# Stacked queries in two buffers in turn from the 17th pair on, with their split written half a step earlier

## Chip, cores and metric

The kernel runs on one core of one Trainium2 chip. The metric is the device time of one execution in microseconds (us). The kernel before takes 730.91 us (median of three executions, 730.74 to 735.16).

## What is computed

Windowed attention with a few sink positions, followed by a gated feed-forward layer. There are 4 batches, 8 heads, 768 positions and 64 numbers per head; a query sees the first 4 positions and the last 128 up to its own. In short:

```
scores = q @ k^T / 8                      # per batch and head, 768 x 768
keep   = (col < n_sink) | (0 <= row - col < window)
a      = softmax(where(keep, scores, -1e9))
x      = (a @ v) laid out as 3072 x 512
h      = x @ w_in                         # 3072 x 2048
out    = (h * clip(h + 3, 0, 6) / 6) @ w_out
```

## The kernel before

**Tiling.** The tokens are cut into 12 units of 256 positions (4 batches, 3 units each; the first unit of every batch comes first). A unit has 4 pairs of heads, so 48 pairs, numbered s = 0 to 47 below; the 17th pair is s = 16. For one pair TensorE computes four score blocks (two heads h, two halves t of 128 queries; `C_score`, L293), VectorE (DVE) masks them and takes the minimum, ScalarE (ACT) does the exponentials and the scaling (`C_soft`), TensorE transposes the probabilities (`D_pt`) and multiplies them with v (`E_av`). When the four pairs of a unit are done, the unit's feed-forward steps go into a queue: for each of 8 slices of the hidden layer two steps of 12 matmuls (`ffn1`, L467, into `hps`), and a slice later two steps of 6 wider matmuls (`ffn2`, L487, into `o`); at the end two steps (`ffn_out`) that hold no matmul, only a copy on ACT and a store. Between the two kinds of matmul the activation runs as a chain: ACT `gf` (L473), DVE `gf` (L474), DVE `gh` (L41), DVE `g` (L476).

**Split numbers.** TensorE reads rounded 32-bit numbers, so operands are split into a high and a low part. For the queries of pair s, `B_q` (L266) lets ACT write the high part and DVE the low part into `qt` (one buffer), and then four DMAs on SyncE's queue (SP) stack the parts of each head on top of each other in the tile `Q` (one buffer, L272). `B_k` (L253) does the same for the keys: `kt`, and four larger DMAs into `K` (one buffer). The score matmuls of pair s read K and Q of pair s. Pairs 0 to 9 take another, plain path without Q and K. The raw queries `qr` and keys `kr` have two buffers each and are loaded from HBM one step ahead by `A_kq`.

**What sets the order.** One list, `ORDER` (L564), is run once per step s: "V" loads and splits v, C00 to C11 are the four scores of pair s-1, E0 and E1 the products with v of pair s-2, "L" loads q and k of pair s+1, "Bk" and "Bq" stack the keys and queries of pair s, D0, D1 and S are transposes for pair s-1. Each "-" takes one step from the feed-forward queue, so there are eight of them in a pair. That is the written order; the framework that builds the program then places ready work of one engine ahead of work that isn't ready, so that an engine's final order differs a little from the written one. Each engine and SP's queue work strictly in their final order, and a DMA waits on SP's queue until its source is written and its destination is free.

**Buffers that matter here.** `Q` and `K` of pair s can only be written when the last score of pair s-1 (C11) has read the old ones. `qt` can only be written again when the four DMAs that read it have landed. The tag `st` (three buffers of 4 KB per partition) holds the staged weights at the start, up to step 11, and afterwards only the output tile `ost` of `ffn_out` (L492).

Of the kernel before, what the change touches and what calls it, by code (L numbers as in the profile page):

```python
# [10 lines left out]
F32R = mybir.dt.float32r  # L11
# [7 lines left out]
P = 128  # L19
# [7 lines left out]
def split_parts(nc, hi, lo, src, hi_engine, lo_engine):  # L27

    copy_r(nc, hi_engine, hi, src)
    lo_engine.tensor_tensor(out=lo, in0=src, in1=hi.bitcast(F32), op=ALU.subtract)  # L30
# [14 lines left out]
def attn_ffn_kernel(ctx: ExitStack, tc: tile.TileContext, qx, kx, vx, vfx, vsx, n_sink, window, w_in, w_out, out):  # L45
# [4 lines left out]
    H, D, UT = 2 * NP, 64, 256  # L50
    S = NU * UT
# [5 lines left out]
    work = fast.enter_context(tc.tile_pool(name="work", bufs=2))  # L57
# [125 lines left out]
    def later_constants():  # L183

        bias_from(m_t0[:, 0:P], prev, nc.gpsimd)
        bias_from(m_t0[:, P:2 * P], own, nc.gpsimd)
        bias_from(m_t0[:, 2 * P:W2], snk[:, 0:SK], nc.gpsimd)
        nc.gpsimd.tensor_copy(out=m_t1[:, 0:P], in_=m_t0[:, 0:P])
        nc.gpsimd.tensor_copy(out=m_t1[:, P:P + SK], in_=m_t0[:, 2 * P:W2])
        nc.gpsimd.tensor_copy(out=m_t1[:, P + SK:W2], in_=m_t0[:, P:2 * P])  # L190
        nc.gpsimd.memset(pz.bitcast(F32), 0.0)
# [15 lines left out]
    def eng(which, s):  # L207
        return {"D": nc.vector, "P": nc.gpsimd, "A": nc.scalar}[which[1 + (s % (len(which) - 1)) if s < START else 0]]
# [16 lines left out]
    def plain(s):  # L225
        return s < NF32 and pus[s][1] == 0
# [26 lines left out]
    def B_k(s):  # L253
# [9 lines left out]
                                  in_=kt[D * h:D * (h + 1), :, 0:w].bitcast(F32))  # L263
        st_[s]["K"] = K

    def B_q(s):  # L266
        if plain(s):
            return
        d = st_[s]
        qt = work.tile([P, 2, UT], F32R, name="qt", bufs=1)  # L270
        split_parts(nc, qt[:, 0, :], qt[:, 1, :], d["qr"], eng(QHI, s), eng(QLO, s))
        Q = work.tile([P, 2, UT], F32R, name="Q", bufs=1)  # L272
        for h in range(2):
            for r in range(2):
                nc.sync.dma_start(out=Q[D * r:D * (r + 1), h, :].bitcast(F32),
                                  in_=qt[D * h:D * (h + 1), r, :].bitcast(F32))
        d["Q"] = Q

# [14 lines left out]
    def C_score(s, h, t):  # L293
# [15 lines left out]
        else:  # L309
            K, Q = d["K"], d["Q"]  # L310
            for part in range(2):
                nc.tensor.matmul(out=sp[:, 0:w], lhsT=Q[:, h, t * P:(t + 1) * P],  # L312
                                 rhs=K[:, h, part, k0c:k0c + w], start=(part == 0), stop=(part == 1))
# [198 lines left out]
    NS = len(pus)  # L512
    queues = []

    def drain(n):

        for _ in range(n):
            live = [q for q in queues if q]
            if not live:
                return  # L520
            if live[0] is queues[0] and len(live) > 1:
                order = live[0:2]
            else:
                order = live[0:1]
            for q in order:
                if q[0][0] <= 4 * NFP - len(w_order):
                    q.pop(0)[1]()
                    break
# [16 lines left out]
    def slot_C(s, h, t):  # L545
        if 0 <= s < NS:
            C_score(s, h, t)
            if t == 1:
                C_soft(s, h)
                if s == 0 and h == 1:  # L550
                    keep_busy(WARM[1])
                elif 0 < s < NP:
                    keep_busy(WARM[2])
# [7 lines left out]
                dsts = [out[r0 + P * tt:r0 + P * (tt + 1), :] for tt in range(2)]  # L561
                queues.append(ffn_steps(units.index((b, u)), xt[(b, u)], work, ps, ps, dsts, "bank"))

    ORDER = "V C00 - C01 - C10 - C11 E0 L - Bk E1 - Bq W - D0 - D1 S -"  # L564
    MULT = [1] * 12
    WN = [0, 1, 1, 1, 1, 4, 4, 4, 4, 4, 4, 4]

    for s in range(NS + 2):
        if s == 3:
            later_constants()  # L570
        for step in ORDER.split():
            if step == "-":
                drain(MULT[s] if s < len(MULT) else 1)
            elif step[0] == "C":
                slot_C(s - 1, int(step[1]), int(step[2]))
            elif step[0] == "E":
                slot_E(s - 2, int(step[1]))
            elif step == "V":
                if s < NS:
                    A_v(s)  # L580
                if 2 <= s and pus[s - 2][1:] == (1, 0):
                    batch_loads(pus[s - 2][0])
            elif step == "L" and s + 1 < NS and s > 0:
                A_kq(s + 1)
            elif step == "Bk" and 0 < s < NS:
                B_k(s)
            elif step == "Bq" and 0 < s < NS:
                B_q(s)
            elif step == "W":
                for _ in range(WN[s] if s < len(WN) else 0):  # L590
                    with ExitStack() as behind:
                        if s <= 5:
                            at = max(min(s, NP) - 2, 0)
                            behind.enter_context(tc.issue_after(st_[at]["min"].ins))
                            behind.enter_context(tc.issue_after(st_[at]["exp"].ins))
                        w_order.pop(0)()
            elif step[0] == "D" and 0 <= s - 1 < NS:
                D_pt(s - 1, int(step[1]))
            elif step == "S" and 0 <= s - 1 < NS:
                D_snk(s - 1)  # L600
# [169 lines left out]
```

## Time and profile before

| | |
|---|---|
| median of three executions | 730.91 us (730.74 to 735.16) |
| the profiled execution, its own time | 730.63 us |
| its span (first to last instruction) | 728.9 us |
| TensorE matmul busy | 709.6 us, 97% of the span |
| DVE busy | 495.4 us, 68% |
| ACT busy | 426.3 us, 58% |
| DMA: K stacking, Q stacking | 152 issues each |

The profile is one execution, taken by the hardware profiler. PE is TensorE's matmul side and PEld its weight loads; SPq is SyncE's DMA queue. A number in square brackets behind a row of a timeline is the time in which the engine sat idle before that instruction, with the name of what ended the wait. A matmul's shown length is longer than the distance at which matmuls follow each other, because they are pipelined: a wait of PE is best read from the distance between two starts.

### The profile page before, as it was taken

To read this page: it belongs to the slowest core of one execution; us is meant where nothing else is said; L and a number is where in the kernel's file an instruction comes from. 1 tells how busy PE (TensorE), PEld (TensorE's weight loads), DVE (VectorE), ACT (ScalarE), POOL (GpSimd) and SP (SyncE) were. 2 spreads that over 40 slices of the span, in tenths; PEclk is the share of its full clock that TensorE was granted. 3 is DMA by queue.
4 is the path that set the end of the run, shared out by engine and by line. 5 is a ranking of instruction groups with operands and counts; after the bars stand their busy time and mean duration, and the time that the engine had idled before them with its cause. 6 is when DMAs were issued, how large, how long until landed. Compare 5 with 4: busy or idle time off the path is not lost.

```text
span 728.9 us, 14295 instructions
## 1 busy us (share of the span) xinstructions
PE 709.6 (97%) x4772; PEld 635.8 (87%) x4772; DVE 495.4 (68%) x1418; ACT 426.3 (58%) x1139; POOL 169.6 (23%) x336
## 2 busy tenths in 40 slices
PE   8997999999999999999999999999999999999996
PEld 7776788998999998999898899999899899899995
DVE  5798999666876766876866876776776775533321
ACT  6988997656566656665555665755655754311111
POOL 1000000000233433433443343353343342100000
PEclk9999999999999999999999999999999999999999
DMA  7656583535546436436445635545635522000000
GB/s 238 196 185 229 194 255 93 152 89 137 146 103 174 116 97 178 127 96 166 115 106 129 175 97 126 152 108 136 167 99 129 150 72 61 30 1 1 30 1 33
DMA packets 55601, 89.11 MB, mean 122 GB/s; under 512 B 8416, under 2 KB 38368, under 8 KB 55520
## 3 DMA queue, kind: packets, MB, share of 16 engines
q1 hardware_dynamic: 55376, 88.11, 44.1%
q8 instruction: 40, 0.66, 0.4%
q14 instruction: 41, 0.34, 0.1%
q10 hardware_dynamic: 144, 0.00, 0.0%
HBM read 42.47 MB, written 6.29 MB: 67 GB/s over the span
## 4 chain that ended last, share of the span: by engine, by line
PE 79%; DVE 7%; ACT 5%; DMA 5%; issue 2%; SPq 1%; POOL 0%; ACTq 0%; DVEq 0%; POOLq 0%
PE hps L467 32%; PE o L487 31%; PE av L429 6%; PE sp L312 5%; PE pt L362 3%; DMA K<-kt 2%; PE sp L307 2%; SPq L262 1%; DMA Q<-qt 1%; DVE gf L474 1%; DVE g L476 1%; ACT Pt L336 1%; DMA st<-in_w_out_dram 1%; ACT gf L473 1%; PE idle L81 1%
## 5 line engine op out<-in xcount | busy, mean ns | idle before, releaser
L467 PE MATMUL hps<-xh,wih 128*128 128x256 f32 x768 | 220.8, 288 | 3.5 <-DVE st L160 2.3
L467 PE MATMUL hps<-xh,wil 128*128 128x256 f32 x768 | 217.3, 283 | 0.2 <-DVE wil L165 0.2
L467 PE MATMUL hps<-xl,wih 128*128 128x256 f32 x768 | 216.1, 282 | 0.1
L487 PE MATMUL o<-woh,gh 128*128 128x512 f32 x384 | 155.1, 404 | 3.7 <-DVE gh L41 3.6
L487 PE MATMUL o<-woh,g 128*128 128x512 f32 x384 | 152.2, 399 | 0.8 <-DVE g L476 0.4
L467 PEld LDWEIGHTS hps<-xh,wih 128*128 128x128 f32 x768 | 144.7, 188 | 8.1 <-ACT wih L35 5.9
L487 PE MATMUL o<-wol,gh 128*128 128x512 f32 x384 | 151.4, 394 | 0.0
L467 PEld LDWEIGHTS hps<-xl,wih 128*128 128x128 f32 x768 | 144.9, 189 | 1.1 <-DVE xl L445 0.3
L467 PEld LDWEIGHTS hps<-xh,wil 128*128 128x128 f32 x768 | 144.4, 188 | 0.9 <-DVE wil L165 0.4
L336 ACT ACTIVATE Pt<-Pt,nb 128x272 f32<-128x272 f32 (+2 forms) x152 | 77.0, 507 | 74.0 <-DVE nb L314 73.0
L344 POOL TENSOR_TENSOR Pt<-Pt 128x256 f32<-128x256 f32 x64 | 47.3, 739 | 276.0 <-ACT Pt L336 276.0
L473 ACT ACTIVATE gf<-hps,three 128x512 f32<-128x512 f32 x96 | 65.4, 682 | 77.1 <-PE hps L467 76.4
L474 DVE SCALAR_TENSOR_TENSOR gf<-gf,hps 128x512 f32<-128x512 f32 x96 | 65.9, 686 | 62.6 <-ACT gf L473 59.5
L487 PEld LDWEIGHTS o<-woh,g 128*128 128x128 f32 x384 | 72.2, 188 | 20.7 <-DVE g L476 4.7
L487 PEld LDWEIGHTS o<-woh,gh 128*128 128x128 f32 x384 | 72.4, 189 | 15.6 <-DVE gh L41 3.8
L487 PEld LDWEIGHTS o<-wol,gh 128*128 128x128 f32 x384 | 72.5, 189 | 10.5
L322 ACT ACTIVATE Pt<-Pt,rc 128x144 f32<-128x144 f32 (+2 forms) x152 | 55.7, 414 | 43.2 <-POOL Pt L344 38.9
L476 DVE TENSOR_TENSOR g<-gf,gh 128x512 fp32r<-128x512 f32 x96 | 68.8, 716 | 1.2 <-PE o L487 0.3
L380 POOL TENSOR_SCALAR_AFFINE_SELECT ph<-ph 128x256 fp32r<-128x256 f32 x64 | 32.5, 512 | 155.7 <-ACT ph L35 155.7
L314 DVE CUSTOM_DVE_ANT_0 Pt<-sp,m_t 128x272 f32<-128x272 f32 x128 | 54.8, 432 | 17.8 <-PE sp L312 15.8
L312 PE MATMUL sp<-K,Q 128*128 128x272 f32 (+2 forms) x304 | 61.7, 287 | 2.0 <-DMA Q<-qt 1.9
L312 PEld LDWEIGHTS sp<-K,Q 128*128 128x128 f32 x304 | 51.5, 189 | 9.7 <-DMA Q<-qt 1.2
(96 smaller groups left out, 1079.3 us busy)
## 6 DMA issues: line engine op xcount, KB each, us to landing
K<-kt SPq DMA_DIRECT2D x128, 200.0 KB, 3.5
Q<-qt SPq DMA_DIRECT2D x152, 64.0 KB, 2.5
st<-in_w_in_dram SPq DMA_DIRECT2D x16, 512.0 KB, 4.1
st<-in_w_out_dram SPq DMA_DIRECT2D x16, 512.0 KB, 4.9
kr<-in_kx_dram SPq DMA_DIRECT2D x32, 200.0 KB, 2.5
qr<-in_qx_dram SPq DMA_DIRECT2D x48, 128.0 KB, 2.2
out_dram<-ost SPq DMA_DIRECT2D x24, 256.0 KB, 2.4
vr<-in_vx_dram SPq DMA_DIRECT2D x32, 192.0 KB, 2.6
```

Source lines behind the costliest of these rows:

```text
L312: nc.tensor.matmul(out=sp[:, 0:w], lhsT=Q[:, h, t * P:(t + 1) * P], rhs=K[:, h, part, k0c:k0c + w], start=(part == 0), stop=(part == 1))
L314: d["min"] = nc.vector.tensor_tensor_reduce(out=cell(s, h, t, 0, w), in0=sp[:, 0:w], in1=m[:, 0:w], scale=-SCALE, scalar=3.0e38, op0=ALU.a ...
L322: nc.scalar.mul(out=blk, in_=blk, mul=c)
L336: d["exp"] = nc.scalar.activation(out=blk, in_=blk, func=AF.Exp, scale=-1.0, bias=nb[:, i:i + 1], accum_out=sm[:, i:i + 1])
L344: nc.gpsimd.tensor_tensor(out=both, in0=both, in1=prior, op=ALU.add)
L380: nc.gpsimd.affine_select(out=prior[i], in_=own[i], pattern=[[0, 2], [-1, P]], base=0, channel_multiplier=1, compare_op=ALU.is_gt, fill=0.0)
L429: nc.tensor.matmul(out=o, lhsT=l, rhs=r, start=(j == 0 and (h == 0 or not plain(s))), stop=(j == len(seq) - 1 and (h == 1 or not plain(s))))
L467: nc.tensor.matmul(out=hp[:, half, :], lhsT=l, rhs=r, start=(j == 0), stop=(j == n - 1))
L473: nc.scalar.activation(out=gf, in_=hp, func=AF.Relu, bias=three, scale=1.0)
L474: nc.vector.scalar_tensor_tensor(out=gf, in0=gf, scalar=6.0, in1=hp, op0=ALU.min, op1=ALU.mult)
L476: eng(GLO, state["n"] * NP).tensor_tensor(out=g, in0=gf, in1=gh.bitcast(F32), op=ALU.subtract)
L487: nc.tensor.matmul(out=acc, lhsT=l[:, f, ts_], rhs=r[i][:, f, :], start=(i == 0 and f == 0 and j == 0), stop=(i == NFP - 1 and f == 1 and ...
```

## The change

From step 16 on the queries' split and stacking is written at a new place in the step, "Bf", between the first and the second score of the pair ahead, instead of "Bq" behind the key stacking and the first product with v. And from pair 17 on the odd pairs' stacked queries lie in a buffer of the tag `st` (named `Q2`), the even ones in `Q` as before. `qt`, K and everything else stay as they are. In the changed file the lines behind the edit stand six lines lower.

```diff
+    QTWO = 16
+
     def B_q(s):
         ...
-        Q = work.tile([P, 2, UT], F32R, name="Q", bufs=1)
+        if s >= QTWO and s % 2:
+            Q = work.tile([P, 512, 2], F32R, tag="st", name="Q2", bufs=3).rearrange("p n w -> p (n w)")[
+                :, 0:2 * UT].rearrange("p (h t) -> p h t", h=2)
+        else:
+            Q = work.tile([P, 2, UT], F32R, name="Q", bufs=1)
         ...
-    ORDER = "V C00 - C01 - C10 - C11 E0 L - Bk E1 - Bq W - D0 - D1 S -"
+    ORDER = "V C00 - Bf C01 - C10 - C11 E0 L - Bk E1 - Bq W - D0 - D1 S -"
         ...
-            elif step == "Bq" and 0 < s < NS:
+            elif step == ("Bf" if s >= QTWO else "Bq") and 0 < s < NS:
                 B_q(s)
```

TensorE's and GpSimd's order are the same before and after. On the other queues the moved split lands at other places; three of them follow. First SP's queue around pair 32, before the change (Q_5333 and K_5483 are those of pairs 31 and 32, Q_5509 and Q_5714 the queries of pairs 32 and 33):

```order
L275 DMA Q_5333<-qt_5330 64x256 x4
L247 DMA vr_5403<-in_vx_dram 128x384
L232 DMA kr_5664<-in_kx_dram 128x400
L233 DMA qr_5665<-in_qx_dram 128x256
L262 DMA K_5483<-kt_5480 64x800 x4
L494 DMA out_0_dram<-ost_5503 128x512
L275 DMA Q_5509<-qt_5506 64x256 x4
L494 DMA out_0_dram<-ost_5514 128x512
```

The same place after the change (K_5312 and K_5491 are the keys of pairs 31 and 32, Q_5424 the queries of pair 32, Q2_5604 those of pair 33):

```order
L262 DMA K_5312<-kt_5309 64x800 x4
L281 DMA Q_5424<-qt_5421 64x256
L247 DMA vr_5403<-in_vx_dram 128x384
L281 DMA Q_5424<-qt_5421 64x256 x3
L232 DMA kr_5672<-in_kx_dram 128x400
L233 DMA qr_5877<-in_qx_dram 128x256
L262 DMA K_5491<-kt_5488 64x800 x4
L500 DMA out_0_dram<-ost_5511 128x512
L500 DMA out_0_dram<-ost_5514 128x512
L247 DMA vr_5576<-in_vx_dram 128x384
L281 DMA Q2_5604<-qt_5601 64x256 x4
```

The queries of pair 32 are stacked a whole pair earlier, behind the keys of pair 31, and behind the keys of pair 32 now stand the queries of pair 33.

Second, DVE around the first score of pair 32, before the change (`sp` is the score in PSUM, `Pt` the probabilities, the two L314 rows the masking and its minimum, `gf`, `gh`, `g` the feed-forward's activation, kt_5675 and qt_5711 the splits of pair 33):

```order
L30 TENSOR_TENSOR kt_5675<-kr_5470,kt_5675 128x400
L474 SCALAR_TENSOR_TENSOR gf_5570<-gf_5570,hps_5528 128x512
L314 ISA Pt_5580,nb_5581<-sp_5584,m_t0_98 128x272
L314 ISA nb_5581 128x1
L41 CAST gh_5569<-gf_5570 128x512
L476 TENSOR_TENSOR g_5568<-gf_5570,gh_5569 128x512
L30 TENSOR_TENSOR qt_5711<-qr_5471,qt_5711 128x256
```

And after the change:

```order
L30 TENSOR_TENSOR kt_5683<-kr_5478,kt_5683 128x400
L320 ISA Pt_5580,nb_5581<-sp_5584,m_t0_98 128x272
L320 ISA nb_5581 128x1
L480 SCALAR_TENSOR_TENSOR gf_5570<-gf_5570,hps_5528 128x512
L41 CAST gh_5569<-gf_5570 128x512
L482 TENSOR_TENSOR g_5568<-gf_5570,gh_5569 128x512
L320 ISA Pt_5580,nb_5581<-sp_5609,m_t1_99 128x272
```

The score's minimum now stands ahead of the activation, and the low part of the queries is gone from this place.

Third, ACT around pair 21, before the change (`gf<-hps` is the first step of the feed-forward's activation):

```order
L35 ACTIVATE qt_3563<-qr_3313 128x256
L473 ACTIVATE gf_3431<-hps_3389,three_75 128x512
L336 ACTIVATE Pt_3441,sm_3443<-Pt_3441,nb_3442 128x272 x2
L322 ACTIVATE Pt_3441<-Pt_3441,rc_3444 128x144 x2
L336 ACTIVATE Pt_3441,sm_3443<-Pt_3441,nb_3442 128x272 x2
L322 ACTIVATE Pt_3441<-Pt_3441,rc_3444 128x144 x2
```

And after the change:

```order
L35 ACTIVATE qt_3654<-qr_3520 128x256
L479 ACTIVATE gf_3431<-hps_3389,three_75 128x512
L342 ACTIVATE Pt_3441,sm_3443<-Pt_3441,nb_3442 128x272 x2
L35 ACTIVATE qt_3830<-qr_3719 128x256
L328 ACTIVATE Pt_3441<-Pt_3441,rc_3444 128x144 x2
L342 ACTIVATE Pt_3441,sm_3443<-Pt_3441,nb_3442 128x272 x2
L328 ACTIVATE Pt_3441<-Pt_3441,rc_3444 128x144 x2
```

Two splits stand in this pair now, those of pairs 23 and 24, and none in pair 22; the second stands between the exponentials of the first head and their scaling.

## Rows read from the trace of the kernel before

**Rows 1.** The page, parts 1 and 2: busy time of the engines, and TensorE's granted clock in 40 slices of the span, in tenths of full speed.

```profile
PE 709.6 (97%) x4772; PEld 635.8 (87%) x4772; DVE 495.4 (68%) x1418; ACT 426.3 (58%) x1139; POOL 169.6 (23%) x336
...
PEclk9999999999999999999999999999999999999999
```

**Rows 2.** Windows (us from the span's start): busy time of PE, PEld, DVE, ACT and POOL in each, then the granted TensorE clock, the DMA engines' busy share and GB/s.

```profile
395.00:405.00 10.00, 8.96 (x66) 8.14 (x66) 6.65 (x21) 6.97 (x19) 4.12 (x9) 1.00 0.64 163
218.00:228.00 10.00, 9.74 (x67) 8.71 (x66) 7.24 (x22) 6.67 (x20) 3.55 (x8) 1.00 0.67 180
245.00:259.00 14.00, 14.00 (x101) 12.88 (x99) 9.99 (x30) 8.33 (x25) 5.11 (x10) 1.00 0.46 116
```

**Rows 3.** Waits of PE in the whole span: who waited for whom, us in total, times, longest.

```profile
PE o L487 <- DVE gh L41: 3.6, 6, 1.4
...
PE sp L312 <- DMA Q<-qt: 1.9, 3, 1.0
...
PE o L487 <- DVE g L476: 0.4, 2, 0.2
```

**Rows 4.** The page, part 6: DMA issues by kind, their number, KB each, median us from issue to landing.

```profile
K<-kt SPq DMA_DIRECT2D x128, 200.0 KB, 3.5
Q<-qt SPq DMA_DIRECT2D x152, 64.0 KB, 2.5
```

**Rows 5.** Timeline of SP's queue around pair 32: start, us, what.

```profile
396.70 2.44 SPq L262 DMA_DIRECT2D K<-kt  x4
399.24 0.80 SPq L494 DMA_DIRECT2D out_dram<-ost  x1
400.09 2.82 SPq L275 DMA_DIRECT2D Q<-qt  x4
```

**Rows 6.** Timeline of PE around the first score of pair 32 and the feed-forward step behind it.

```profile
402.33 0.28 PE L467 MATMUL hps<-xl,wih 128*128 128x256 f32 x1
402.45 0.28 PE L467 MATMUL hps<-xh,wil 128*128 128x256 f32 x1
403.76 0.48 PE L312 MATMUL sp<-K,Q 128*128 128x272 f32 x2 [1.03 <-DMA Q<-qt]
...
407.44 0.40 PE L487 MATMUL o<-woh,gh 128*128 128x512 f32 x1
...
407.92 0.39 PE L487 MATMUL o<-woh,g 128*128 128x512 f32 x1
```

**Rows 7.** The tile K from 396 to 403 us, that is, the four stacking DMAs of pair 32's keys: us from issue to landing.

```profile
DMA to landing us min/median/max: 2.6/3.4/4.0
```

**Rows 8.** Timeline of PE at the first score of pair 19.

```profile
224.41 0.30 PE L391 MATMUL spt<-ident_r,ssc 128*128 128x128 f32 x1
224.97 0.49 PE L312 MATMUL sp<-K,Q 128*128 128x272 f32 x2 [0.26 <-DMA Q<-qt]
```

**Rows 9.** Timeline of PE at the first score of pair 36.

```profile
457.28 0.30 PE L391 MATMUL spt<-ident_r,ssc 128*128 128x128 f32 x1
457.58 0.49 PE L312 MATMUL sp<-K,Q 128*128 128x272 f32 x2
```

**Rows 10.** Timeline of PE where nothing is waited for behind such an `spt`.

```profile
280.00 0.31 PE L391 MATMUL spt<-ident_r,ssc 128*128 128x128 f32 x1
...
280.14 0.44 PE L487 MATMUL o<-woh,gh 128*128 128x512 f32 x1
```

**Rows 11.** Timeline of DVE around the first score of pair 32.

```profile
404.43 0.77 DVE L30 TENSOR_TENSOR kt<-kr,kt 128x400 fp32r<-128x400 f32 x1
405.12 0.68 DVE L474 SCALAR_TENSOR_TENSOR gf<-gf,hps 128x512 f32<-128x512 f32 x1
405.71 0.43 DVE L314 CUSTOM_DVE_ANT_0 Pt<-sp,m_t 128x272 f32<-128x272 f32 x1
...
406.07 0.42 DVE L41 CAST gh<-gf 128x512 fp32r<-128x512 f32 x1
406.53 0.69 DVE L476 TENSOR_TENSOR g<-gf,gh 128x512 fp32r<-128x512 f32 x1
```

**Rows 12.** Timeline of ACT in pair 21: the split, the feed-forward's activation, the second exponential, the first scaling.

```profile
252.87 0.42 ACT L35 ACTIVATE qt<-qr 128x256 fp32r<-128x256 f32 x1
253.58 0.69 ACT L473 ACTIVATE gf<-hps,three 128x512 f32<-128x512 f32 x1 [0.29 <-PE hps L467]
...
256.08 0.53 ACT L336 ACTIVATE Pt<-Pt,nb 128x272 f32<-128x272 f32 x1 [0.98 <-DVE nb L314]
...
257.55 0.72 ACT L322 ACTIVATE Pt<-Pt,rc 128x144 f32<-128x144 f32 x2 [0.85 <-POOL Pt L344]
```

**Rows 13.** Timeline of DVE in pair 21: the low part of the split, and the activation's `gh`.

```profile
253.32 0.64 DVE L30 TENSOR_TENSOR qt<-qr,qt 128x256 fp32r<-128x256 f32 x1
...
255.03 0.66 DVE L41 CAST gh<-gf 128x512 fp32r<-128x512 f32 x1
```

**Rows 14.** Timeline of PE: the first matmul that reads that `gh`.

```profile
261.30 0.40 PE L487 MATMUL o<-woh,gh 128*128 128x512 f32 x1
```

**Rows 15.** Timeline of PE behind the first score of pair 28, at the end of a unit.

```profile
348.48 0.50 PE L487 MATMUL o<-woh,gh 128*128 128x512 f32 x1 [0.47 <-DVE gh L41]
```

**Rows 16.** The tile Q in the whole span: us from issue to landing of its 152 DMAs.

```profile
DMA to landing us min/median/max: 2.0/2.5/5.1
```

## Prediction

> **What bounds the kernel now.** I read the page first: TensorE's matmul side is busy 97% of the span, DVE 68%, ACT 58%, and the granted clock is at full speed (the 2.4 GHz level) in all 40 slices [rows 1]. So only what PE waits for can be won. The windows show where that is: a pair in the middle of a unit has PE busy 14.00 of 14.00 us, while a stretch at the end of a unit has 8.96 of 10.00 [rows 2]. The reason is in the code: the two steps of `ffn_out` hold no matmul, so at the end of each unit PE runs through two of its eight feed-forward slots at once and comes to the next pair's first score sooner than usual. Third, PE's waits over the whole span: 3.6 us for `gh`, 1.9 us for the stacking of the queries, 0.4 us for `g` [rows 3]. That is all that this change can touch: some 6 us of 731, or 0.8%.
>
> **What the change removes.** Before, the queries' four DMAs stand behind the keys' four on SP's queue, and the keys' wait for the last score of the pair ahead. In pair 32 the keys are issued from 396.70 for 2.44 us, the queries from 400.09 for 2.82 us [rows 5]; with 2.5 us from issue to landing [rows 4] the part that the first score needs arrives between 403 and 404. PE's last matmul ahead of it starts at 402.45, the distance between two such matmuls is 0.12 us (402.33 to 402.45), so the score could start at 402.57; it starts at 403.76, waiting for Q [rows 6]. Lost: 403.76 - 402.57 = 1.19 us. The same at pair 19: 224.97 - 224.41 = 0.56 us from `spt` to the score [rows 8], where 0.14 us is the distance without a wait (280.14 - 280.00) [rows 10]; lost 0.42 us. At pair 36 it is 457.58 - 457.28 = 0.30 us [rows 9], lost 0.16. What is left of the 1.9 us of [rows 3], 1.9 - 1.03 - 0.26 = 0.6 us by the idle times in brackets [rows 6, 8], is pair 15's, ahead of step 16, and stays. Sum: 1.19 + 0.42 + 0.16 = 1.77 us.
>
> From pair 17 on the queries of a pair are stacked right behind the keys of the pair ahead, or sooner, so they have landed long before. All 1.77 us of waiting for Q go.
>
> **What is late next: the keys.** They keep their single buffer and their place behind the last score of the pair ahead. In pair 32 the last of the four issues starts at about 396.70 + 2.44 - 0.61 = 398.5 (a quarter of 2.44 is 0.61); the slowest of the four took 4.0 us to land [rows 7], so all are there at 402.5 at the latest, and PE arrives at 402.57. The margin is next to nothing, but it holds, and the next pair's queries, now behind the keys, take nothing from them on the queue. I set this at 0. If the keys came 0.5 us later at the three places, 1.5 us of the 1.77 would be given back; if the emptier queue makes them land at their 3.4 us median [rows 7], nothing is.
>
> **What is late after that: DVE at pair 32.** While PE waited there, DVE caught up. Its row of work runs from `kt` (404.43) over `gf` (405.12) to `gh` (406.07, 0.42 us long) and `g` (406.53, 0.69 us) [rows 11]. PE reads that `gh` at 407.44 and `g` at 407.92 [rows 6]; 1.19 us sooner would be 406.25 and 406.73. In the new order the minimum of the score (0.36 us from 405.71 to 406.07) stands ahead of `gf`: `gf` starts at 405.12 + 0.36 = 405.48, `gh` about 0.70 later at 406.2 and ends at 406.6, `g` ends about 407.3. So PE waits 0.35 us for `gh` and, reaching `g` at 406.73 + 0.35 = 407.08, about 0.25 us for `g`. Given back: 0.6 us. Bounds: 0 if `kt` comes sooner too, 1.19 if all the saved time is waited for here.
>
> **What the moved split costs.** The work is the same: per pair one ACT instruction of 0.42 us [rows 12], one DVE instruction of 0.64 us [rows 13], four DMAs of 2.82 us on SP [rows 5]. Two places of it matter.
>
> In the middle of a unit mostly two splits now stand in one pair and none in the next, and the second waits until the DMAs of the first have landed, since `qt` has one buffer. In pair 21 the second one's place on ACT is behind the exponential of 256.08, where ACT sits idle until 257.55 anyway for GpSimd [rows 12]. The first split's low part ends at 253.96 on DVE [rows 13], four issues of 0.7 us and a landing of 2.0 to 2.5 us (5.1 at most) [rows 4, 16] bring 253.96 + 2.1 + 2.1 to 2.5 = 258.2 to 258.6: the scaling is late by about 1.1 to 1.5 us with the copy of 0.42. Does PE see it? The feed-forward chain has room there: `gh` ends at 255.69 [rows 13] and is read at 261.30 [rows 14], 5.6 us later. So nothing on the path; if the cover were gone, 1.5 us at each of some seven pairs, 10 us.
>
> At the ends of units there is no such room: behind pair 28's first score PE waits for `gh` itself [rows 15]. A split that newly stands ahead of a chain there costs up to 0.42 + 0.64 = 1.06 us, one that leaves such a place gives as much back. By the new order of ACT and DVE some leave (pairs 32, 44) and one comes (pair 40, the second of its head's scalings). I take 0, with bounds of -1.5 (a good third of the 3.6 + 0.4 us of [rows 3]) and +2.5 (two or three places at 1.06 us). The buffers of the tag `st` cost nothing: the staged weights are done by step 11, and an `ost` comes only twice in four pairs.
>
> **A rule against it.** In the windows with the longest of these waits, 395 to 405, the granted clock is 1.00, the same as where PE never waits [rows 2]. The Trainium skill, in TensorE: Matmul & The Clock Gate, section What's actually happening, says that the slow clock is the default and that activity releases it, so a PE that pauses may fall to half rate. By that rule new waits would cost far more than their length; by the rows none of this size did, and I leave the clock out of the sum.
>
> **The sum.** 730.63 (the profiled execution) - 1.77 + 0.6 = 729.46 us. That execution lies 0.28 us under the median of 730.91, so on the median's scale 729.7 us, 0.2% faster: too little to be told from no change, since about 1% (7.3 us) is what a measurement of this kernel can tell.
>
> **The rivals.**
> - *The keys take the queries' place, or DVE takes all of it* (0.20). For it: the margin of 0.07 us in pair 32, and that DVE was the late one there. Against it: at pair 19 neither holds. Time 730.4 to 731.4: a change that does nothing.
> - *The moved splits hold up the feed-forward chain at unit ends* (0.09): slower. Its place is `gh` behind a unit's end, where there is no room [rows 15]; eight units end from step 16 on. At 1.06 us each it is 8.5 us less the 1.77 won: 730.91 + 6.7 = 737.6. It passes 1% only if a split also waits for a landing there, 2.5 us [rows 4] at four places or more, 10 us and up. Against it: only one split newly comes to such a place. Over 1%: 0.03.
> - *Waits at unit ends go too* (0.05), because some splits leave those places: 1.77 plus 2 of the 4 us of [rows 3], 727.1 us. More than 1% faster would need every wait of [rows 3] and more: 0.01.
> - *The clock falls* (0.01). A pair of 14 us [rows 2] at half rate costs 14 us more: 745. The skill's page named above is what speaks for it, the clock of [rows 2] against it.
> - *The forecast* (0.65): 728.9 to 730.6.
>
> **Numbers.** Prediction 729.7 us. For 8 in 10 the range runs from 727.6 (all of 1.77 kept, and the bound of -1.5 at the unit ends) to 733.2 (nothing kept, and +2.3 at the unit ends); the cases outside it are the upper part of the slower rival, the clock, and the lower end of the faster one. Faster by over 1%: 0.01; within 1%: 0.95; slower by over 1%: 0.04.
>
> **What would show it.** Right: in the table of PE's waits Q is left with pair 15's alone; at pairs 19, 32 and 36 the score follows at 0.12 to 0.14 us; behind pair 32's score a new wait of some 0.6 us for `gh` and `g`; ACT waits for Q's landing in about every second pair, with no wait of PE behind it. Wrong: PE waits for K at a pair's first score (first rival), or PE's wait for `gh` grows from 3.6 us to 8 or more (second), or windows with a clock under 1.00 (fourth).

## The result, and the profile after

| | before | after |
|---|---|---|
| median, us (executions) | 730.74 (5) | 736.35 (5) |
| lowest and highest, us | 730.26, 735.16 | 735.18, 740.15 |
| profiled execution: time, span, us | 730.63, 728.9 | 736.35, 734.7 |
| mean granted clock of that execution | 0.999 | 0.994 |

The change made the kernel 0.77% slower: ratio 1.0077, interval 1.0053 to 1.01. Measured once more on another occasion (the run a2_after below) it was 1.0055, 1.0026 to 1.0083. The forecast was 729.7 us with a range to 733.2.

The page of the changed kernel, parts 1 and 5, cut to what answers to [rows 1, 3] (idle time before the group and its releaser stand last):

```profile
PE 712.7 (97%) x4772; PEld 638.1 (87%) x4772; DVE 493.3 (67%) x1418; ACT 423.9 (58%) x1139; POOL 168.5 (23%) x336
...
L493 PE MATMUL o<-woh,gh 128*128 128x512 f32 x384 | 155.8, 406 | 7.1 <-DVE gh L41 6.9
L493 PE MATMUL o<-woh,g 128*128 128x512 f32 x384 | 152.8, 400 | 1.2 <-DVE g L482 1.0
...
L318 PE MATMUL sp<-K,Q 128*128 128x272 f32 (+2 forms) x304 | 61.5, 287 | 0.7 <-DMA Q<-qt 0.7
```

The waits for the stacked queries went from 1.9 to 0.7 us, as intended. Those for `gh` went from 3.6 to 6.9 and those for `g` from 0.4 to 1.0. Of the 3.6 us in [rows 3], 2.2 lie ahead of 130 us, where the change touches nothing; from there to the end the kernel before (first line) and the changed one (second line) have these (total, times, longest):

```profile
PE o L487 <- DVE gh L41: 1.4, 4, 0.5
```

```profile
PE o L493 <- DVE gh L41: 4.7, 6, 2.0
```

ScalarE's splits wait for landings far more often than the 2.5 us in three places of the kernel before, none of them behind 195 us (waits of ACT in the changed kernel from 130 us to the end):

```profile
ACT qt L35 <- DMA Q<-qt: 22.3, 23, 2.7
```

Where the time went is read best from one event that every pair has, the start of its first score. The table is worked out from the two traces (start in the changed kernel less start in the kernel before, us; a2_after is a second profile of the changed kernel):

```
pair              18     19     28     32     33     39     40     44     45     47   end of span
after            1.78   1.36   1.28   0.10   0.86   0.68   3.66   3.83   4.79   5.32   5.73
a2_after         4.08   3.66   3.62   2.45   3.19   3.01   4.61   4.73   5.67   6.19   6.13
```

Up to 177 us, ahead of pair 16, ACT, DVE and SP have the same instructions in the same order in both kernels. At pair 16 the difference is already 1.78 (4.08) us, and it stays that to pair 18, so these are not the change's. From pair 18 to pair 39 the changed kernel gains 1.10 (1.07) us, as the prediction's sum has it; between pairs 39 and 40 it loses 2.98 (1.60), from pair 40 to 47 another 1.66 (1.58). Together the change costs 3.54 (2.11) us from pair 18 to 47. Behind the last matmul the end of the span moves by itself, by 0 to 1.6 us in the runs below, with no matmul in that stretch.

**Pair 40.** SP's queue in the changed kernel, start and length (us): the keys of pair 39, one of the four transfers of pair 40's queries, the raw values of pair 40, and only then the other three.

```profile
492.08 2.45 SPq L262 DMA_DIRECT2D K<-kt  x4
494.58 0.81 SPq L281 DMA_DIRECT2D Q<-qt  x1
498.32 0.33 SPq L247 DMA_DIRECT2D vr<-in_vx_dram  x1
498.69 1.74 SPq L281 DMA_DIRECT2D Q<-qt  x3
```

Between the first and the second transfer of Q lie 4.11 us. `vr` has one buffer; its load waits 2.8 us, until VectorE has split pair 39's values (at 498.3), and three transfers stand behind it. ScalarE at the same place:

```profile
499.75 0.52 ACT L400 CAST pz<-spt 64x128 fp32r<-64x128 f32 x2
502.99 0.42 ACT L35 ACTIVATE qt<-qr 128x256 fp32r<-128x256 f32 x1 [2.73 <-DMA Q<-qt]
503.44 0.69 ACT L479 ACTIVATE gf<-hps,three 128x512 f32<-128x512 f32 x1
```

The split of pair 41's queries stands ahead of the relu; in the kernel before, the split at that place is pair 40's and waits for nothing (it starts at 499.61, the relu at 500.32). Here it waits 2.73 us, because the one buffer of `qt` is read by pair 40's late transfers. The relu, both heads' exps and the next relu (510.90, before 508.61) follow late, `gh` with them (513.48, before 511.19), and TensorE, which has no other work there, waits:

```profile
511.53 0.38 PE L368 MATMUL pt<-ident_r,Pt 128*128 128x128 f32 x2
513.96 0.50 PE L493 MATMUL o<-woh,gh 128*128 128x512 f32 x1 [2.04 <-DVE gh L41]
514.29 0.44 PE L493 MATMUL o<-wol,gh 128*128 128x512 f32 x1
514.89 0.80 PE L493 MATMUL o<-woh,g 128*128 128x512 f32 x1 [0.16 <-DVE g L482]
515.49 0.63 PE L493 MATMUL o<-woh,gh 128*128 128x512 f32 x1
515.91 0.63 PE L493 MATMUL o<-wol,gh 128*128 128x512 f32 x1
516.34 0.63 PE L493 MATMUL o<-woh,g 128*128 128x512 f32 x1
```

The last three follow each other at 0.42 us, where 0.24 is the distance in the second profile below. The windows of this profile (busy time of PE, PEld, DVE, ACT, POOL; granted clock; DMA share; GB/s) show why:

```profile
64.00:66.00 2.00, 1.69 (x8) 1.70 (x9) 2.00 (x6) 0.99 (x3) 0.00 (x0) 0.50 0.79 250
66.00:68.00 2.00, 2.00 (x10) 1.43 (x9) 1.58 (x3) 2.00 (x5) 0.00 (x0) 0.66 0.37 100
512.00:514.00 2.00, 0.04 (x1) 0.05 (x1) 1.94 (x6) 0.52 (x1) 0.00 (x0) 1.00 0.00 0
514.00:516.00 2.00, 1.84 (x5) 1.17 (x6) 1.94 (x5) 1.46 (x4) 0.00 (x0) 0.63 0.35 98
516.00:518.00 2.00, 2.00 (x8) 1.60 (x7) 1.45 (x5) 1.08 (x4) 1.53 (x4) 0.52 0.49 135
518.00:520.00 2.00, 2.00 (x14) 1.79 (x13) 0.82 (x4) 0.87 (x3) 1.66 (x5) 1.00 0.59 186
```

Behind the idle stretch the granted clock fell to 0.5 of full speed, that is from the 2.4 to the 1.2 GHz level, and from 518 on it is 1.00 again. It also fell at 64 to 68 us, at the end of a wait of 2.46 us for the weights (2.27 us in the kernel before, without a fall); there the two kernels have the same instructions in the same order.

### The profile page after: what moved, and what is told of

It is laid out like the page before. It is cut to its first block, busy times and chain, and to the rows that moved or that the text cites. A ratio compares the mean times of both kernels' runs of the same rounds, so it can differ in the third digit from the quotient of the medians.

```text
span 734.7 us, 14286 instructions
## 1 busy us (share of the span) xinstructions
PE 712.7 (97%) x4772; PEld 638.1 (87%) x4772; DVE 493.3 (67%) x1418; ACT 423.9 (58%) x1139; POOL 168.5 (23%) x336
## 4 chain that ended last, share of the span: by engine, by line
PE 72%; DVE 9%; ACT 7%; DMA 5%; issue 2%; POOL 2%; SPq 1%; DVEq 0%; ACTq 0%; POOLq 0%
PE o L493 29%; PE hps L473 29%; PE av L435 6%; PE sp L318 4%; DMA K<-kt 3%; PE pt L368 3%; PE sp L313 1%; DVE gf L480 1%; ACT Pt L342 1%; ACT Pt L328 1%; POOL Pt L350 1%; DVE st L160 1%; DVE wt L162 1%; ACT gf L479 1%; SPq L262 1%
```

## The experiments

All were timed beside the kernel before on the same chip. Its own executions spread from 729.4 to 736.9 us, and the mean granted clock goes with it: 0.997 to 0.999 near 731, 0.990 to 0.994 near 735. So each run is read by its ratio, by the table of pairs of its profile, and by the clocks of its executions (last column: how many are at 0.995 or under). The mean clock also counts the stretch behind the last matmul, where the clock falls in every profile; in `e1_place` that alone makes 0.996.

```
run           median  ratio  interval          pair 18   39     40     44     47   end   clock<=0.995
before                                                                                  20 of 77
after         736.35  1.0077 1.0053 to 1.01     1.78   0.68   3.66   3.83   5.32   5.73   5 of 5
a2_after      736.44  1.0055 1.0026 to 1.0083   4.08   3.01   4.61   4.73   6.19   6.13  10 of 12
e2_buffer     734.1   1.0057 1.0031 to 1.0082   0.36  -0.67   0.26   0.36   0.81   1.30   7 of 10
e1_place      735.88  1.0059 1.0036 to 1.0082  -0.18   1.47   1.48   2.21   3.14   4.75   0 of 7
e4_vr         732.45  1.0013 0.9992 to 1.0035  -0.31  -1.28  -1.29  -1.16   0.01   0.20   4 of 10
e3_qt         731.52  1.0001 0.9977 to 1.0025   0.08  -0.92  -0.42  -0.30   0.28   1.15   1 of 10
e8_relu       731.37  0.9993 0.9972 to 1.0014   1.70   1.44   1.50   1.33   1.23   1.81   3 of 10
e10_until     729.92  0.997  0.9949 to 0.9991   0.77  -0.24  -0.25  -0.23  -0.22   0.08   2 of 12
e12_from41    733.76  1.0036 1.001 to 1.0061   -0.80  -0.87  -0.88   0.17   1.64   1.88   4 of 12
e6_fill       738.74  1.0088 1.0058 to 1.0118   0.10   2.48   5.09   6.06   7.53   8.16   0 of 6
e6b_fill8     738.0   1.0069 1.0041 to 1.0098   0.19   2.35   3.69   4.74   6.23   6.50   1 of 9
```

**The two halves.** First the second buffer alone (the split written at its old place), then the place alone (one buffer):

```diff
-            elif step == ("Bf" if s >= QTWO else "Bq") and 0 < s < NS:
+            elif step == "Bq" and 0 < s < NS:
```

> The change's second buffer alone: the queries' split is written at the place it had in the kernel before, and the pairs of odd number from the 17th on have their stacked queries in a buffer of the tag st. The theory: the loss sits at pairs 39 and 40, where, in the trace of the changed kernel, ScalarE's split of pair 41's queries waits 2.73 us for the landing of pair 40's (502.89 us) and the feed-forward's relu, the scores' exps and with them gh stand behind it; the second buffer is what lets pair 41's split stand there, so this kernel loses as the change does: 735 to 736.5 us, with a wait of TensorE of about 2 us for gh near 513 us. The first rival (the moved place costs): without the place the loss goes and the removed waits of 1.77 us stay won, 729 to 731 us. The second rival (a fall of the granted clock near 64 us, ahead of the change, is most of it): 731 to 732.7 us, with or without that fall in the profile, and no wait over 1 us for gh near 513.

```diff
-        if s >= QTWO and s % 2:
-            Q = work.tile([P, 512, 2], F32R, tag="st", name="Q2", bufs=3).rearrange("p n w -> p (n w)")[
-                :, 0:2 * UT].rearrange("p (h t) -> p h t", h=2)
-        else:
-            Q = work.tile([P, 2, UT], F32R, name="Q", bufs=1)
+        Q = work.tile([P, 2, UT], F32R, name="Q", bufs=1)
```

> The change's place alone: from step 16 the queries' split comes behind the second score of the pair ahead, and the stacked queries keep their one buffer. The theory (the second buffer lets a split wait in front of the feed-forward's chain): the split of pair 41 stands behind that chain's relu here and waits in front of nothing that is due, so no wait over 1 us for gh near 510 us; the waits for the stacked queries at pairs 19, 32 and 36 stay (1.77 us), and the time is that of before, 730 to 732 us. The first rival (the moved place costs): 735 to 736.5 us. The second rival (clock ahead of the change): 730.7 or 732.7 us as the profile shows the fall near 64 us or not.

The buffer alone does bring the wait at pair 40: its ScalarE and SP have the order shown above, although the split was written at its old place. The loss is smaller than expected, 0.93 us at pair 40 and, with the waits that it wins, 0.45 us from pair 18 to 47. The rest of its 0.57% has to lie in the other executions, seven of ten with a clock at 0.995 or under; where their falls lie no profile shows. ScalarE and TensorE at pair 40:

```profile
500.97 0.42 ACT L35 ACTIVATE qt<-qr 128x256 fp32r<-128x256 f32 x1 [2.06 <-DMA Q<-qt]
```

```profile
511.92 0.50 PE L493 MATMUL o<-woh,gh 128*128 128x512 f32 x1 [1.36 <-DVE gh L41]
```

The place alone was a miss of the theory, which had 730 to 732 us. It costs as much as the change, and not by the clock, which is at 0.996 to 0.999 in all seven executions. With one buffer the next pair's queries can't be stacked before the last score of the pair ahead is done, and on SP they now stand in front of the next keys (in the order of SP four Q of pair 40, then four K, where before it is K and then Q). TensorE's waits from 180 us on (total, times, longest):

```profile
PE o L489 <- DVE g L478: 2.8, 5, 0.9
PE sp L314 <- DMA K<-kt: 1.5, 2, 0.8
PE o L489 <- DVE gh L41: 1.0, 2, 0.7
```

ScalarE's splits wait for landings here too, 21.7 us in 25 places, so the earlier place brings such waits without a second buffer. The change is not the sum of its halves: 0.57% and 0.59% alone, 0.55 to 0.77% together. Where the waits for `g` come from in the order of VectorE was not followed further.

**The wait for the landing, taken away in two ways.** Both kernels are the changed one with more room at one place; the orders of the queues shift a little elsewhere too. First the raw values get three buffers, so that their load no longer stands between the transfers of Q:

```diff
-        vr = work.tile([P, 3, 2, D], F32, name="vr", bufs=1)
+        if s >= QTWO:
+            vr = work.tile([P, 512], F32, tag="wt", name="vr2", bufs=3)[:, 0:3 * 2 * D].rearrange(
+                "p (s h d) -> p s h d", s=3, h=2)
+        else:
+            vr = work.tile([P, 3, 2, D], F32, name="vr", bufs=1)
```

> The changed kernel with a second and third buffer for the raw values from step 16 (they take buffers of the tag wt, which the weights no longer use). On the queue of SP pair 40's values then no longer wait for the split of pair 39's between the first and the second transfer of pair 40's queries; in the trace of the changed kernel that put 4.1 us between them (494.58 and 498.69 us). The theory: the four transfers follow each other near 494.6 us and have landed by about 499, ScalarE's split of pair 41 then waits for nothing when it is due near 500.3, TensorE's wait for gh near 511 falls from 2.04 to about 0.6 us and the clock stays up behind it: about 3 us less than the change, 732 to 733.5 us. The first rival (the extra split in front of the chain costs by its place in the order, whatever it waits for): 735 to 737 us, with gh waits as in the change. The second rival (clock ahead of the change is most): 734 to 736.5 with the fall near 64 us in the profile, and about 2 less without it, whatever stands near 511.

SP's queue, ScalarE and TensorE at the same place (start, length, and in brackets the idle time):

```profile
490.12 2.43 SPq L266 DMA_DIRECT2D K<-kt  x4
492.60 3.02 SPq L285 DMA_DIRECT2D Q<-qt  x4
496.23 0.33 SPq L251 DMA_DIRECT2D vr<-in_vx_dram  x1
```

```profile
498.33 0.42 ACT L35 ACTIVATE qt<-qr 128x256 fp32r<-128x256 f32 x1
499.04 0.69 ACT L483 ACTIVATE gf<-hps,three 128x512 f32<-128x512 f32 x1 [0.29 <-PE hps L477]
```

```profile
510.39 0.50 PE L497 MATMUL o<-woh,gh 128*128 128x512 f32 x1 [0.44 <-DVE gh L41]
```

The split stands at the same place in the order of ScalarE, but it waits for nothing, the wait for `gh` is that of the kernel before (0.43 us there), and pair 40 loses 0.01 us instead of 1.6 to 3.0. That speaks against the first rival: at this place a copy ahead of the relu costs nothing, a copy that waits does. Then three buffers for the split queries themselves:

```diff
-        qt = work.tile([P, 2, UT], F32R, name="qt", bufs=1)
+        if s >= QTWO:
+            qt = work.tile([P, 2, UT], F32R, tag="wt", name="qt2", bufs=3)
+        else:
+            qt = work.tile([P, 2, UT], F32R, name="qt", bufs=1)
```

> The changed kernel with three buffers (of the tag wt) for the split queries from step 16, so that no split waits for the landing of the previous pair's stacked queries. The order of ScalarE then has the splits about three pairs further ahead. The theory (the wait for the landing, in front of the feed-forward's chain, is the loss): ScalarE shows no wait for a landing of the queries, TensorE's wait for gh near 511 us is 0.6 us or under, and the time 731.5 to 733.5 us. The first rival (an extra split ahead of a relu costs by itself): the splits stand ahead of other work now and the sum of the waits for gh stays at 5 to 7 us, 734 to 737 us. The second rival (the transfers' order on the queue of SP, where pair 40's queries still have the values between them, makes the stacked queries late for the first score): a wait of 0.5 us or more for the stacked queries at some pair, 732 to 735 us.

The time is that of the kernel before, in the theory's range. But the theory wanted no wait of ScalarE for a landing, and there still are some: the splits moved three pairs ahead, pair 43's now stands in front of that relu, and it waits 1.64 us for a landing (8.7 us in 8 waits in all, where the changed kernel has 22.3 in 23). Pair 40 loses 0.50 us.

**Holding the split back.** The changed kernel, with ScalarE's part of the split queued behind the relu written last before it:

```diff
+    last = {}
     ...
-        split_parts(nc, qt[:, 0, :], qt[:, 1, :], d["qr"], eng(QHI, s), eng(QLO, s))
+        with ExitStack() as behind:
+            if s >= QTWO:
+                behind.enter_context(tc.issue_after(last["relu"].ins))
+            split_parts(nc, qt[:, 0, :], qt[:, 1, :], d["qr"], eng(QHI, s), eng(QLO, s))
     ...
-            nc.scalar.activation(out=gf, in_=hp, func=AF.Relu, bias=three, scale=1.0)
+            last["relu"] = nc.scalar.activation(out=gf, in_=hp, func=AF.Relu, bias=three, scale=1.0)
```

> The changed kernel with each split of the queries from step 16 on held behind the feed-forward's relu that was written last before it, on ScalarE, in issue order alone. The split of pair 41 then stands behind the relu near 509 us, not ahead of the exps near 503. The theory: no wait over 1 us for gh near 511, the clock stays up there, and the time is 731 to 733.5 us; the waits for the stacked queries at pairs 19, 32 and 36 may come back in part, since the splits are later. The rival (the change costs by the place of the copies on VectorE, behind the relu, as in the kernel with the place alone, 735.88 us): waits for g of 0.8 us and more near 291, 514 and 526 us, and 734.5 to 736.5 us.

No loss at pair 40 (0.06 us) and none behind it, as the theory had it. But pair 33 gives back 1.37 us where the change gives back 0.76, so that only 0.47 us are left from pair 18 to 47; within the interval that is no change.

**The clock.** The changed kernel again, and then with matmuls that nobody reads in the stretch in which TensorE waits at pair 39:

> The changed kernel once more, unaltered, to see in more executions how often the granted clock falls. Its first profile has two falls to about half: at 64 to 67 us, behind a wait of 2.46 us for the weights in a part in which the two kernels have the same instructions in the same order, and at 514 to 518 us, behind the wait of 2.04 us for gh. The theory: the second fall comes in every execution (the wait is made by the change), the first one in some, as in the kernel before (whose mean clock was 0.99 to 0.995 in 5 of 28 executions and 0.997 to 0.999 in the rest); so the mean clock is 0.996 or less in all, and the time 733.5 to 737 us, lower where the profile shows no fall near 64. The rival (the change makes the first fall too): every execution at 0.995 or less, 735 to 740 us, and the fall near 64 is in the profile again. The other rival (the first comparison had chance executions): about 731 us at 0.998.

The profile of this execution has the same wait of 2.04 us, and no fall behind it; the matmuls go on at 0.24 us:

```profile
513.86 0.38 PE L368 MATMUL pt<-ident_r,Pt 128*128 128x128 f32 x2
516.28 0.50 PE L493 MATMUL o<-woh,gh 128*128 128x512 f32 x1 [2.04 <-DVE gh L41]
516.62 0.40 PE L493 MATMUL o<-wol,gh 128*128 128x512 f32 x1
517.22 0.50 PE L493 MATMUL o<-woh,g 128*128 128x512 f32 x1 [0.20 <-DVE g L482]
517.55 0.39 PE L493 MATMUL o<-woh,gh 128*128 128x512 f32 x1
517.79 0.39 PE L493 MATMUL o<-wol,gh 128*128 128x512 f32 x1
```

So "in every execution" was wrong, and the two profiles part the price: the wait costs 1.60 us, the fall behind it 2.98 - 1.60 = 1.38 more. The one execution at 0.999 took 733.04 us; as far as one execution can tell, that is the changed kernel without falls, some 2 us over the kernel before. The other 3.3 to 3.4 us of its two medians go with a lower clock. One fall as at pair 39 takes about 0.002 off the mean clock (an estimate: the windows at 0.63 and 0.52 miss 1.7 us of 734.7), and 11 of the 17 executions lie at 0.994 or under, before 18 of 77; so from the usual 0.997 to 0.999 most have more than that one fall. Both profiles have one near 64 us (in this execution it lasts from 64 to 75 us, and 4.08 us are lost by pair 18), ahead of all that the change touches. So the rival that the change makes the first fall too is not ruled out: why the changed kernel has it so often, where its instructions are those of the kernel before, stays open.

```diff
+        if s == 39 and h == 0:
+            for _ in range(17):
+                nc.tensor.matmul(out=pt[:, 3 * P:4 * P], lhsT=relf[:, 0:P], rhs=relf[:, 0:P], start=True, stop=True)
```

> The changed kernel with 17 matmuls of 128 by 128 whose results nobody reads, into an unused part of pt, behind the transposes of pair 39 and in front of the matmuls that wait for gh near 514 us; by the 0.115 us that such a matmul takes at its pace in the warm-up they fill 1.95 us of the 2.2 us wait. The order of the other instructions around pair 39 is that of the changed kernel. The theory (half the loss at pair 40 is the clock that falls behind the idle wait): gh comes as late as before, but the clock stays at 1.00 behind it, and the first score of pair 40 comes 0.9 to 1.7 us earlier than in the changed kernel, measured against the first score of pair 39; 734.0 to 735.5 us with the fall near 64 us, 732.3 to 733.7 without. The rival (the wait alone is the loss): no gain, pair 40 is 2.9 us or more behind the kernel before, 735 to 737 us.

This tells little: each of these matmuls is two records, so that the 17 took 3.71 us and held TensorE past `gh`; pair 40 loses 2.61. The same with 8:

> The changed kernel with 8 matmuls whose results nobody reads in front of the matmuls that wait for gh at pair 39, in place of the 17 of the kernel before this one: there the trace showed that each of them is two records of 0.109 us (34 in 3.71 us), so that 17 held TensorE 1.7 us past gh. Eight take 1.75 us of a wait of 2.2. That kernel also had an order of its own ahead of pair 39, with waits for the sinks' values at pairs 26 and 34 that cost 1.9 and 1.5 us against the changed kernel; they come again, so the time is judged by pair 40 against pair 39 and by the mean clocks. The theory (the fall of the clock follows the idle stretch; the wait itself costs about 1.6 us, as in the second profile of the changed kernel, in which the clock stayed up): pair 40 loses 1.5 to 1.8 us against pair 39, no fall near 515 us in the profile, and mean clocks of 0.997 and more in two executions of three, as in the kernel before, where the changed kernel had 0.995 or less in 15 of 17; 735.5 to 737.5 us. The rival (the falls come from something else in the change): mean clocks of 0.995 and less in most executions, 738 us and more.

```profile
513.20 0.38 PE L368 MATMUL pt<-ident_r,Pt 128*128 128x128 f32 x2
513.42 1.95 PE L371 MATMUL pt<-rel 128*128 128x128 f32 x16
515.36 0.50 PE L496 MATMUL o<-woh,gh 128*128 128x512 f32 x1
```

Pair 40 loses 1.34 us, no fall is in the profile, and one execution of nine is at 0.995 or under, where the changed kernel has 15 of 17. It fits the theory, but does not prove it alone: this kernel also has another order in the first 70 us, where the other falls were seen, and the time is worse for the waits at pairs 26 and 34 that this order brings.

**Where in the program.** The change up to pair 36 alone, and the change from pair 41 on alone:

```diff
-    QTWO = 16
+    QTWO, QEND = 16, 37
...
-        if s >= QTWO and s % 2:
+        if QTWO <= s < QEND and s % 2:
...
-            elif step == ("Bf" if s >= QTWO else "Bq") and 0 < s < NS:
+            elif step == ("Bf" if QTWO <= s < QEND else "Bq") and 0 < s < NS:
```

> The change only up to the 36th pair: second buffer and new place from step 16 to 36, and from 37 on the one buffer and the old place, so that the orders of ScalarE, VectorE and SP are those of the changed kernel up to pair 36 and those of the kernel before behind it. The theory (the loss sits at pairs 39 to 46, the won waits at pairs 19, 32 and 36): the first score of pair 36 is 1.1 us earlier than in the kernel before (as in the changed kernel, where it went from 1.78 late at pair 18 to 0.71 at pair 36), pair 40 loses nothing, the ends of units behind it take up to 0.7 of it back; 729.4 to 730.7 us, which would be the first version faster than the kernel before. The rival (the loss is a cost of the change in all of its length, in SP's queue or the clock ahead of it): 732 to 735 us.

This is the version that beats both: ratio 0.997, interval 0.9949 to 0.9991. Part of that is the clock, since two of its 12 executions lie at 0.995 or under and 10 of the 29 beside it; over the others the medians are 729.76 and 731.21 us, 0.2% apart. From pair 18 to 39 it gains 1.01 us, and pairs 40 to 47 lose 0.02 of it. TensorE's waits from 505 us to the end (total, times, longest) are these, where the changed kernel has 1.5 us for `gh` and 0.5 for `g` from 519 us alone, besides the 2.04 us of pair 39:

```profile
PE o L493 <- DVE gh L41: 1.1, 3, 0.4
PE o L493 <- DVE g L482: 0.2, 1, 0.2
```

```diff
-    QTWO = 16
+    QTWO = 41
```

> The change from the 41st pair on alone (the step's bound is 41 in place of 16), so that the orders of ScalarE, VectorE and SP are those of the kernel before up to pair 40. The theory (two places lose: pair 40, by the split that waits for a landing, and the ends of units at pairs 44 to 46, where the feed-forward's chain through ScalarE and VectorE is slower in the new order or simply later than TensorE): no loss at pair 40 here; pairs 45 and 46 lose 0.8 to 1.5 us against pair 44, and nothing is won: 731.7 to 732.7 us beside a kernel before at 730.7 to 731.5. If they lose nothing here, TensorE was only earlier at that chain in the kernel with the third buffer of the values (0.49 to 1.16 us ahead of before), and the change's 1.5 us there is a follow-up of pair 40's loss, not an order of its own: 730.5 to 731.5 us.

Nothing is lost at pair 40, and 2.52 us from there to pair 47 (0.44 at pair 41, 0.61 by pair 44, 1.47 at 45 and 46, as expected). The median lies above the expected time, with four of 12 executions at 0.995 or under; the profiled one took 732.51 us. So the ends of units behind pair 40 lose by something of their own, not as a sequel of pair 40. The waits of TensorE and ScalarE behind 511 us:

```profile
PE o L493 <- DVE gh L41: 2.0, 4, 0.9
PE o L493 <- DVE g L482: 0.8, 3, 0.3
PE sp L318 <- DVE gf L480: 0.4, 1, 0.4
```

```profile
ACT qt L35 <- DMA Q<-qt: 4.1, 3, 1.8
```

*Pair 45* loses 0.94 us here and 0.96, 0.94 and 0.67 in after, a2_after and e4_vr. In these four profiles (and in the two with idle matmuls) pair 46's split stands in pair 43 ahead of the scaling and the relu and waits there for a landing: 1.81 us here, then 1.42, 1.35 and 1.05. ScalarE in pair 43, first in e4_vr (its first score starts at 554.15), where three buffers of the values shorten that wait but don't end it, then in the kernel before (first score 555.31):

```profile
558.43 0.42 ACT L35 ACTIVATE qt<-qr 128x256 fp32r<-128x256 f32 x1 [1.05 <-DMA Q<-qt]
558.75 0.71 ACT L332 ACTIVATE Pt<-Pt,rc 128x144 f32<-128x144 f32 x2
559.49 0.69 ACT L483 ACTIVATE gf<-hps,three 128x512 f32<-128x512 f32 x1
```

```profile
558.87 0.69 ACT L473 ACTIVATE gf<-hps,three 128x512 f32<-128x512 f32 x1 [0.33 <-PE hps L467]
```

The relu comes 5.34 us behind the first score, before 3.56. In e2_buffer, e3_qt and e8_relu no split stands there, the relu comes at 3.56 us, and pair 45 loses nothing (-0.06, 0.05 and -0.10); e1_place, with orders of its own, loses 0.47 there and at pair 46. So this loss goes with a split that waits for a landing ahead of a relu. With it the scaling changes places with the relu, though, and no run parts the two.

*Pair 46* loses 0.49 to 0.53 us in every profile with the second buffer at that place but e8_relu's, and nothing in e8_relu and e10_until. No split waits ahead of that chain; where it loses, ScalarE has a scaling ahead of two exponentials where the kernel before has the exponentials first, and the relu behind them starts 1.4 us ahead of pair 45's first score in place of 1.9. That this order is the cause is argued from the traces, not shown by a run of its own.

## Why the prediction was wrong, point by point

- *The removed waits, 1.77 us, the keys at 0, and 0.6 us given back at pair 32*: right. Q is waited for at pair 15 alone (0.7 us); pair 32's first score follows the matmul ahead of it at 0.12 us, and by pair 33 0.76 us are given back. The sum was -1.17 us, and from pair 18 to 39 the two profiles have -1.10 and -1.07. The kernel with the change up to pair 36 alone keeps it, with -1.01, and is 0.2 to 0.3% faster. TensorE at pair 32 in the changed kernel:

```profile
403.74 0.28 PE L473 MATMUL hps<-xh,wil 128*128 128x256 f32 x1
403.86 0.41 PE L318 MATMUL sp<-K,Q 128*128 128x272 f32 x2
```

- *In the middle of a unit the second split waits for a landing and nobody sees it*: right; ScalarE has 23 waits of splits for a landing from 130 us on (three in the kernel before), and nothing is lost between pairs 20 and 23, 29 and 31, or 36 and 39.
- *"I take 0, with bounds of -1.5 and +2.5" at the ends of units*: this step failed. Measured without the clock: 1.60 us at pair 40 and 1.6 from there to pair 47, 3.2 us together, outside the bound. I counted the length of a split that newly stands ahead of a chain, 1.06 us, and not its wait. The pieces were on the table: the landing wait was worked out for the middle of a unit, the single buffer of `qt` named, and the second rival says that it decides if a split waits for a landing there. What was not looked at is the queue that the transfers were moved on: SP's new order, shown for pair 32 ahead of the prediction, has the values' load between the first and the second transfer of Q; at pair 40 that was 4.11 us. With the values' buffers taken out of the way pair 40 loses 0.01 us. The lower bound of -1.5 was too wide as well: of the 3.6 + 0.4 us of [rows 3] only 1.8 lie behind 130 us.
- *The second rival* was the right mechanism with too small a chance (0.09): three places instead of eight, pair 40 with a wait for a landing that the runs show, pair 45 with such a wait in the profiles that lose there, pair 46 with an order that is only argued. The rival that waits at unit ends go too, by 2 us, had at most those 1.8 to win.
- *"I leave the clock out of the sum"*: wrong as well. The rows of before had no fall behind waits of about 1 us; the new wait is 2.04 us, and a fall behind it cost 1.38 us, not the 14 us at which the rival of the clock set a fall. The Trainium skill, in TensorE: Matmul & The Clock Gate, section What's actually happening, has the slow clock as the default that activity releases. The falls of the first profile, with waits of 2.04 and 2.46 us, agree with it; the second profile, with the same wait of 2.04 us and the clock at full speed, shows that it need not come. The clock of that profile also stays at 0.50 from 66 to 74 us, although TensorE shows as busy in all of that stretch.
- *The range* ended at 733.2, near the 733.04 us of the one execution without a fall, but for other reasons than those it was set by: it had nothing won and 2.3 us lost at unit ends, where 1.1 us are won and 3.2 lost. What lies above goes with the clock: 1.38 us by the fall at pair 39, the rest by falls of which the two profiles show one near 64 us each, with a cause that stays open. Nor was 1% the least that can be told here: the measured interval, 1.0053 to 1.01, shows 0.77%.

## What to carry to other kernels

A second buffer at the end of a chain of stagings lets the first stage run a pair ahead, and it then waits on the stage that kept one buffer; where such a wait stood in ScalarE's order ahead of work that TensorE needs soon, it cost 0.3 to 0.7 of its length here (0.50 us of 1.64 in e3_qt, 0.67 of 1.05 in e4_vr, 1.60 of 2.75 in a2_after). So follow each moved DMA through the issuing queue, name the load that stands between it and its neighbours, and give the middle stage room, or apply the change only where the stretch behind it has slack. And where a change makes TensorE idle for some 2 us at one place, count the matmuls behind it at half rate as a possible term.

## What the runs showed of the hardware

The granted clock can fall behind an idle stretch of 2.04 us and can stay up behind one of the same length at the same place of the same kernel; what decides was not found. Near 64 us the length of the wait doesn't decide either: with 2.46, 1.93 and 1.72 us it fell (after, e8_relu, a2_after), with 2.27 and 2.13 us it didn't (before, e2_buffer). The profiles of the other runs have no fall there; the instructions and their order are the same there in all but the two kernels with idle matmuls. 20 of 77 executions of the kernel before have a mean clock of 0.995 or under, and every one of the 77 over 733.2 us is among them; where their falls lie no profile shows.
